# When splits, rests of weights and norms are issued between the score phases of a fused attention and MLP kernel

## The chip, the cores and the metric

The kernel runs on one core of one Trainium2 chip. The metric is the device time of one execution in microseconds (us); lower is better. The runs of the kernel before the change took 1242.66 us in the median of three (1241.65 to 1244.49).

## The reference

`x` is [2048, 512]. An attention branch with 32 query heads of 16 that share one key and one value head, and an MLP with a squared ReLU, are mixed by a gate:

```python
q = (x @ wq).reshape(B, S, H, Dh).transpose(0, 2, 1, 3)   # S = 2048, H = 32, Dh = 16
k = x @ wk; v = x @ wv
scores = einsum("bhqd,bkd->bhqk", q, k) * Dh ** -0.5
a = (softmax(scores) @ v, heads side by side) @ wo
h = relu(x @ w1 + b1) ** 2                                # F = 1792
b = h @ w2 + b2
g = sigmoid((x * gate_w).sum(-1, keepdims=True))
out = g * a + (1 - g) * b
```

## The kernel before

**The products.** Every float32 factor of a large product is split in two, a rounded part (`r`) and the rest (`l = f - r`), and a product of 512 columns is summed from the three partial products r·r, l·r and r·l. A *unit* of work is one such product into one bank of PSUM, 12 matmul slots long (9 or 3 for some). `work()` lists the units: the queries (`q_unit`), the MLP's first layer (`hidden`), its second (`summed`), the output projection, and the last chunk's rows (`onto`). Two units run side by side in the two halves of TensorE's rows: the first half of one unit beside the second half of the unit before. Such a pair is a `Span`.

**The attention** is cut into four chunks of 512 queries and eight groups of four heads, which gives 32 iterations `it` of 32 *score units* (128 keys by 256 queries by four heads), 1024 in all. For a score unit TensorE makes the scores (L761). Most go into a tile `s` that ScalarE reads at once (exp, L798). About every fifth goes into the tile `x`, of which there is a single buffer: VectorE copies it out (L782, `e<-x`), and ScalarE takes the exp later. Until the second of a unit's two copies out of `x` is done, no other use of `x` can start, so TensorE stops at its next matmul into `x`.

**The loop** goes `block(u)`, `phase()`, `context()`. `block` chooses how many score units come next: six, or four where a span of 12 slots is cut into two halves. `phase` emits score matmuls and product matmuls (L1102) on TensorE in an order that a table, `PLANS`, gives for the number of units, the slots, and WHOLE, FIRST or SECOND: `M` is a product slot, `S3` the scores of the phase's unit 3 into `s`, `02` one half (0) of unit 2 into `x`, followed by its copy, and `12` the other. `context` then multiplies exponents by values (L812) for units whose scores were made four units before: 24 matmuls for six units, 16 for four. The instructions of each engine run in the order in which this Python code emits them.

**VectorE's order** is set by a planner. `at_pe`, `at_act` and `at_dve` are clocks that it keeps for the three engines with costs written in the code. Ahead of each copy out of `x`, `spend()` puts on VectorE whatever these clocks say has time: the rest of a weight tile that ScalarE has rounded (`w_rest`, L490; ScalarE's rounding is L495, due at `since`), evictions, items of `divisions`, and `chores`. There are 24 divisions for a pair of iterations (bound L826, compare L829, reciprocal L832, product L833, for six parts of the columns), with `at_act + 10` as the time from which they are ready. Chores are the splits of attention rows (load of `stage` from `oTs` on SyncE, L961; cast and rest, L191 and L192) and of other operands. After a chore that issues a load, `held` keeps the next chore back by 6 us of the planner's time.

A weight tile is loaded by `w_load` (L473, SyncE) into one of two places for each layer: `w2f` and a slice of `stage` alternate for the second layer. A tile is rounded by ScalarE (L495) or VectorE (L481). If a unit begins whose tiles aren't there, `have` makes them at once, burst-wise, and loads them first if it must. A hidden unit is evicted in four operations (L660, L661, L191, L192), a summed one in one (L684).

At the end of an iteration `finish` copies the accumulator (L845, ScalarE) and unpacks it by two DMAs on SyncE (L203, L204); when `it` is even, all divisions that are left are put on VectorE at once. At an iteration's start `q_load` issues eight DMAs on SyncE (L433).

**The norms of q.** For each of the chunk's query groups `qnorm` (L412) sums squares by four small matmuls into the bank of `x`; a root (L347, L348) reads them out. It stands at the start of the phase that follows. That happens four times within the loop.

**The tail.** The last pair of iterations is finished by transposes (`turn`, L876 to L885). Where the sequence of units has nothing ready, a span is empty; the start of a span after it makes TensorE wait for a copy of one column (`peek`, L1125).

Of the kernel before, what the change touches and what calls it, by code (L numbers as in the profile page):

```python
# [22 lines left out]
NC, CH = 4, 512  # L23
NG = 8
NK = S // 128
NF = F // 128
# [6 lines left out]
ROOT = float(0x1fbd1df5 + 0x80000)  # L33
WARM = 10
PARTS = [slice(a, min(a + 86, CH)) for a in range(0, CH, 86)]
LANDS, DIVIDES = 6.0, 10.0
PAIR, CONTEXT, TURN, EXP, COPY, LATE = 0.235, 0.429, 0.36, 0.925, 0.66, 0.3
GROUPS = (0, 1, 2, 3), (4, 5, 6, 7), (8, 9, 10), (11, 12, 13)
AHEAD = 4
WHOLE, FIRST, SECOND = range(3)  # L40
PLANS = {
    (6, 12, WHOLE): ("M 02 S0 M S1 M M M M M S3 M M M S4 12 M M S5", (0, 1, 3, 4, 5, 2)),
    (6, 9, WHOLE): ("S0 M 03 M S1 M M M S2 M M M S4 13 M S5", (0, 1, 2, 4, 5, 3)),
    (6, 6, WHOLE): ("S0 M S1 M 03 M S2 M 13 M S4 M S5", (0, 1, 2, 4, 3, 5)),
    (6, 6, SECOND): ("S0 M S1 M 03 M S2 M 13 M S4 M S5", (0, 1, 2, 4, 3, 5)),
# [117 lines left out]
def mix_kernel(ctx: ExitStack, tc: tile.TileContext, xT, wkv, wq, wo, w12, b1, b2, cst, out):  # L163
# [16 lines left out]
    ok = keep.tile([128, NC * KT * len(PARTS)], F32, name="ok")  # L180
# [46 lines left out]
    with fast, tc.tile_pool(name="at", bufs=1) as at, \  # L227
# [249 lines left out]
        def w_round(half, copy):  # L477
            n = len(rounded[half])
            assert n < room[half]
            rounded[half][n] = [at.tile([128, 512], F32R, name=f"w{half + 1}{x}", bufs=3 + half) for x in "rl"]  # L480
            copy(rounded[half][n][0], wf[half][n])  # L481
            if copy == scalar_copy:
                since[half][n] = act(0.64)
            else:
                since[half][n] = dve(0.46)

# [133 lines left out]
        def spend(until=None):  # L620

            nonlocal held

            def fits(d, ready=0.0):
                return until is None or max(at_dve, ready) + d <= until

            while True:
                due = [i for i in halves() if len(rounded[i]) > len(ws[i])]
                if due and fits(0.68, since[due[0]][len(ws[due[0]])]):
                    w_rest(due[0])  # L630
                elif soon and fits(soon[0][1]):
                    dve(soon[0][1])
                    soon.pop(0)[2]()
                elif divisions and fits(*divisions[0][:2]):
                    d, ready, f = divisions.pop(0)
                    dve(d, ready)
                    f()
                elif chores and fits(chores[0][0], held):
                    d, f = chores.pop(0)
                    dve(d, held if d else 0.0)  # L640
                    if f():
                        held = max(at_dve, at_pe) + 6.0
                else:
                    return

# [46 lines left out]
        def x_again(c):  # L692

            r, l = [xp.tile(sh, F32R, name=f"x{n}again{c}", tag=f"x{n}{c - 2}") for n in "rl"]
            def load(a):
                nc.sync.dma_start(stage()[:, :2], xT[c, 2 * a:2 * a + 2].rearrange("k p s -> p k s"))
                return True

            def part(k):
                split(r[:, k], l[:, k], stage()[:, k % 2])  # L700
                if k == KT - 1:
                    x[c] = r, l

# [97 lines left out]
        def context(acc, us):  # L801

            nonlocal at_pe
            at_pe += 0.12
            while us:
                u, (it, kt, q) = us[0], place(us[0])
                n = 2 if u % 2 == 0 and len(us) > 1 and it < NC * NG - 1 else 1
                at_pe = max([at_pe] + [made[i] + 0.06 for i in us[:n]]) + CONTEXT * n
                us = us[n:]
                cols, mine = slice(q * HC, (q + n) * HC), slice(u % 2 * HC, (u % 2 + n) * HC)  # L810
                for h in range(4):
                    nc.tensor.matmul(acc[h * 32:(h + 1) * 32, cols], v_ext[:, kt],  # L812
                                     es[u // 2][:, h % 2 * 2 + h // 2, mine], start=(kt == 0), stop=(kt == NK - 1),
                                     skip_group_check=True, tile_position=(0, h * 32))
            at_pe += 0.24

        ol = {}
# [17 lines left out]
        def finish(it, acc):  # L835

            c, gr = divmod(it, NG)
            t, u = divmod(gr, 2)
            if it == NC * NG - 2:
                a = at.tile([128, CH], F32, name="al", tag="accs")  # L840
                nc.vector.tensor_copy(a, acc)
                side.append(turn(a, 0, range(4), LAST_OK))
                return
            a = at.tile([128, CH], F32, name="accs")
            nc.scalar.activation(a, acc, AF.Copy)  # L845
            act(0.62, at_pe)
            if u == 0:
                while divisions:
                    divisions.pop(0)[2]()
                ol[c, t] = [at.tile([128, CH], F32, name=n) for n in ("oc", "lc")]  # L850
            o, l = ol[c, t]
            unpack(nc.sync, o[u * 64:u * 64 + 64], l[u * 64:u * 64 + 64], a)
            if u == 1:
                for q, cols in enumerate(PARTS):
                    i = len(PARTS) * (4 * c + t) + q
                    divisions.extend((d, at_act + DIVIDES, f) for d, f in divide(o, l, cols, ok[:, i:i + 1]))

                def done():
# [73 lines left out]
        def o_ready(c):  # L932

            if c == 0 and not wos:
                wos.extend(xp.tile(sh, F32R, name=n, tag=t) for n, t in (("wor", "xr2"), ("wol", "xl2")))

                def load(a):
                    nc.sync.dma_start(stage()[:, :2], wo[a * 256:a * 256 + 256].rearrange("(t p) n -> p t n", p=128))
                    return True

                for t in range(KT):
                    if t % 2 == 0:
                        chores.append((0.0, lambda t=t: load(t // 2)))
                    later(split, wos[0][:, t], wos[1][:, t], stage()[:, t % 2])
            if c > 0:
                ask(c - 1)

        def ask(c, n=KT):
            if c in asked or any((c, t) not in complete for t in range(n)) or c > len(asked):
                return  # L950
            if c and not used[c - 1]:
                return
            asked.add(c)
            tiles = []

            def load(a):
                if a == 0:
                    tiles.extend((keep.tile(sh, F32R, name="orr", tag="r3"), xp.tile(sh, F32R, name="orl", tag="xl3")))
                m = min(2, n - 2 * a)
                i = c * NG + 4 * a  # L960
                nc.sync.dma_start(stage()[:, :m], oTs[i:i + 2 * m].rearrange("(t u) d n -> (u d) t n", u=2))  # L961
                return True
# [12 lines left out]
        def ask_one(c, t):  # L975
# [5 lines left out]
            def load():  # L981
                i = c * NG + 2 * t
                nc.sync.dma_start(stage()[:, :1], oTs[i:i + 2].rearrange("(t u) d n -> (u d) t n", u=2))
                return True

            def part():
                split(osp[c][0][:, t], osp[c][1][:, t], stage()[:, 0])
# [141 lines left out]
        def phase(slots, n, m):  # L1129

            nonlocal scored, evicted, at_pe
            step_aside()
            if narrow:
                used_x[0] = dve(1.3) + 0.06
                qnorm(narrow.pop(0))
            if span.done[0] == 0:
                begin()
            kind = SECOND if span.done[0] else WHOLE if slots == span.slots else FIRST
            text, order = PLANS.get((n, slots, kind)) or plain(n, slots)
            rows = [], []  # L1140
            for item in text.split():
# [40 lines left out]
        def block(u):  # L1182
# [15 lines left out]
        halved, units_left = [0.5], [NC * (NF + 16) + 15 + 12]  # L1198

        acc, us = None, ()  # L1200
        fetch()
# [79 lines left out]
```

## Time and profile before

| | |
|---|---|
| Median of three runs | 1242.66 us (1241.65 to 1244.49) |
| The profiled execution's own time | 1243.74 us |
| Span of the profiled execution | 1242.0 us |
| Mean granted clock of TensorE | 0.992 |
| TensorE matmuls (PE) | 1219.7 us busy, 98% of the span |
| ScalarE (ACT) | 1038.9 us busy, 84% |
| VectorE (DVE) | 767.0 us busy, 62% |
| GpSimd (POOL) | 67.3 us busy, 5% |

Since TensorE is nearly always busy, a shared average says little. The places to look at are the few where the start of one context (L812) stands further from the next than the same pair of steps needs elsewhere, and the rows around them: what TensorE waited for (the bracket at a row's end), and what VectorE was doing ahead of the copy that released it.

### The profile page before, as it was taken

Reading aid. Unit: us, or ns where it says so; the run is one execution under the profiler, and the core shown is the slowest. Engines: PE = TensorE matmul, PEld = TensorE weight load, DVE = VectorE, ACT = ScalarE, POOL = GpSimd, SP = SyncE. Lnnn points to the kernel's source line nnn. Section 1 sums busy time; section 2 is a strip of 40 time slices with the busy share of each in tenths; the row PEclk is TensorE's granted clock in tenths of the full one; section 3 lists DMA queues with packets and bytes.
Section 4 is the critical chain, followed back from the end, with each engine's and each line's share of the span. In section 5 each row is a group of like instructions: output and inputs, shape, how many; then the busy total and the mean of one; then the engine's idle time right before and its main releaser. Section 6 shows DMA issues by size and latency. Waiting matters only on the chain.

```text
span 1242.0 us, 24097 instructions
## 1 busy us (share of the span) xinstructions
PE 1219.7 (98%) x9838; PEld 674.0 (54%) x9839; DVE 767.0 (62%) x1507; ACT 1038.9 (84%) x1151; POOL 67.3 (5%) x87
## 2 busy tenths in 40 slices
PE   9999999999999999999999999999999999999997
PEld 4554555555555545555555556555555555554553
DVE  6765667567485854738477674755838577465543
ACT  6788788888898878888798888888888888887864
POOL 1000120000000110000002001000000000000000
PEclk9999999999999999999999999999999999999989
DMA  6334331211213122102124212112112222300011
GB/s 225 85 106 112 91 94 42 65 57 56 64 61 116 56 82 94 58 21 65 56 82 132 77 41 92 46 48 65 62 67 61 73 65 82 90 31 27 23 51 37
DMA packets 45349, 88.72 MB, mean 71 GB/s; under 512 B 10643, under 2 KB 10899, under 8 KB 44721
## 3 DMA queue, kind: packets, MB, share of 16 engines
q1 hardware_dynamic: 37024, 68.27, 18.2%
q0 software_dynamic: 8064, 18.59, 4.7%
q8 instruction: 79, 1.29, 0.5%
q14 instruction: 38, 0.30, 0.1%
q10 hardware_dynamic: 144, 0.26, 0.1%
HBM read 57.83 MB, written 20.97 MB: 63 GB/s over the span
## 4 chain that ended last, share of the span: by engine, by line
PE 90%; ACT 5%; DVE 2%; DMA 1%; issue 1%; SPq 0%; ACTq 0%; DVEq 0%
PE acc L812 35%; PE mm L1102 31%; PE s L761 16%; PE x L761 5%; ACT e L798 4%; DMA stage<-oTs 1%; PE mm L295 0%; DMA qa<-qs 0%; DVE e L782 0%; PE acc L524 0%; PE mm L199 0%; DVE n L832 0%; ACT w1r L495 0%; DVE tmp L347 0%; SPq L433 0%
## 5 line engine op out<-in xcount | busy, mean ns | idle before, releaser
L798 ACT ACTIVATE e<-s 128x1024 f32<-128x1024 f32 x825 | 786.1, 1025 | 176.8 <-PE s L761 158.7
L812 PE MATMUL acc<-e,v_ext 128*32 128x512 f32 (+1 forms) x4224 | 487.4, 590 | 0.0
L782 DVE COPY e<-x 128x512 f32<-128x512 f32 x398 | 274.6, 690 | 329.2 <-PE x L761 284.5
L761 PE MATMUL s<-qa,k_aug 49*128 49x512 f32 x1650 | 466.4, 414 | 1.8 <-ACT e L798 1.2
L761 PEld LDWEIGHTS s<-qa,k_aug 49*128 49x128 f32 x1650 | 235.8, 185 | 79.5 <-ACT e L798 54.5
L812 PEld LDWEIGHTS acc<-e,v_ext 128*32 128x32 f32 x4224 | 117.2, 110 | 244.6 <-issue 241.3
L1102 PE MATMUL mm<-w2r,hr 64*128 64x512 f32 x896 | 228.5, 402 | 0.0
L798 ACT ACTIVATE e<-e 128x1024 f32<-128x1024 f32 x199 | 211.1, 1061 | 0.4 <-DVE e L782 0.4
L761 PE MATMUL x<-qa,k_aug 49*128 49x512 f32 x398 | 162.9, 409 | 7.8 <-DVE e L782 6.1
L1102 PEld LDWEIGHTS mm<-w2r,hr 64*128 64x128 f32 x896 | 136.0, 186 | 46.3 <-DVE hr L192 15.9
L1102 PE MATMUL mm<-w2l,hr 64*128 64x512 f32 x448 | 144.9, 393 | 0.0
L761 PEld LDWEIGHTS x<-qa,k_aug 49*128 49x128 f32 x398 | 74.3, 187 | 52.2 <-issue 10.9
L1102 PEld LDWEIGHTS mm<-w2l,hr 64*128 64x128 f32 x448 | 80.8, 186 | 6.8
L1102 PE MATMUL mm<-xragain,w1r 64*128 64x512 f32 x224 | 76.8, 418 | 0.2
L1102 PE MATMUL mm<-xr,w1r 64*128 64x512 f32 x224 | 74.1, 417 | 0.3
L1102 PE MATMUL mm<-xlagain,w1r 64*128 64x512 f32 x224 | 74.3, 391 | 0.0
L1102 PE MATMUL mm<-xragain,w1l 64*128 64x512 f32 x224 | 73.3, 392 | 0.0
L1102 PE MATMUL mm<-xl,w1r 64*128 64x512 f32 x224 | 72.4, 392 | 0.0
L1102 PE MATMUL mm<-xr,w1l 64*128 64x512 f32 x224 | 71.4, 393 | 0.0
L832 DVE RECIPROCAL n<-n 128x86 f32<-128x86 f32 x90 | 61.5, 684 | 2.0
L1102 PEld LDWEIGHTS mm<-xragain,w1r 64*128 64x128 f32 x224 | 38.4, 185 | 28.5 <-issue 11.7
L1102 PEld LDWEIGHTS mm<-xr,w1r 64*128 64x128 f32 x224 | 37.5, 185 | 27.5 <-issue 10.4
(162 smaller groups left out, 1178.2 us busy)
## 6 DMA issues: line engine op xcount, KB each, us to landing
stage<-in_w SPq DMA_DIRECT2D x56, 256.0 KB
qa<-qs SPq DMA_DIRECT2D x186, 64.0 KB
w1f<-in_w SPq DMA_DIRECT2D x28, 256.0 KB
w2f<-in_w SPq DMA_DIRECT2D x28, 256.0 KB
qs<-qr SPq DMA_DIRECT2D x16, 256.0 KB
ress<-res POOLq DMA_DIRECT2D x4, 1024.0 KB, 4.9
qs<-ql POOLq DMA_DIRECT2D x15, 256.0 KB, 8.7
oc<-accs SPq DMA_DIRECT2D x30, 128.0 KB
```

The lines of the kernel that those rows point to most:

```text
L761: nc.tensor.matmul(dst.rearrange("p (a n) -> p a n", a=2), k_aug[rows, kt * 128:(kt + 1) * 128], qa[it][rows, :, q * HC:q * HC + HC], star ...
L782: nc.vector.tensor_copy(e_half(u)[:, 2 * r:2 * r + 2], x.rearrange("p (a n) -> p a n", a=2))
L798: nc.scalar.activation(e_half(u), src, AF.Exp, scale=SCALE)
L812: nc.tensor.matmul(acc[h * 32:(h + 1) * 32, cols], v_ext[:, kt], es[u // 2][:, h % 2 * 2 + h // 2, mine], start=(kt == 0), stop=(kt == NK ...
L832: return ((0.23, bound), (0.35, compare), (0.72, lambda: nc.vector.reciprocal(n[0], n[0])), (0.28, lambda: nc.vector.tensor_tensor(o[:, co ...
L1102: nc.tensor.matmul((self.before if r else self).bank, a[p], b[p], start=not r and i == 0, stop=r == 1 and i == len(self.terms[1]) - 1, ski ...
```

## The change

Four edits, all in the order of the work:

1. A constant `SURE` = 0.7 is added to the time at which a weight tile rounded by ScalarE is due. Its rest on VectorE is therefore planned later, often behind a copy where it stood ahead of one, and a tile that would have waited for ScalarE may be rounded on VectorE instead.
2. A chore's function returns how long the next chore is held back: 6 us as before for most loads, 10 us for the loads of attention rows in `ask`. The divisions of the pair (chunk 3, pair 2) are ready after 6 us, the others after 10 as before.
3. `qnorm` is emitted at the end of `context()` rather than at the start of the next phase, and that phase, if whole, uses a new plan `LATER`, in which the first matmul into `x` stands seven items later.
4. A span is not cut into halves where ten score units of the iteration pair are left, nor behind a `qnorm`.

```diff
-LANDS, DIVIDES = 6.0, 10.0
+LANDS, DIVIDES, SURE = 6.0, 10.0, 0.7
...
-WHOLE, FIRST, SECOND = range(3)
+WHOLE, FIRST, SECOND, LATER = range(4)
 PLANS = {
     (6, 12, WHOLE): ("M 02 S0 M S1 M M M M M S3 M M M S4 12 M M S5", (0, 1, 3, 4, 5, 2)),
+    (6, 12, LATER): ("S0 M M S1 M M M 02 M S3 M M M S4 M 12 M M S5", (0, 1, 3, 4, 5, 2)),
...
             if copy == scalar_copy:
-                since[half][n] = act(0.64)
+                since[half][n] = act(0.64) + SURE
...
-                    if f():
-                        held = max(at_dve, at_pe) + 6.0
+                    wait = f()
+                    if wait:
+                        held = max(at_dve, at_pe) + wait
...
+            if narrow:
+                at_pe = max(at_pe + 0.2, used_x[0] + 0.05)
+                qnorm(narrow.pop(0))
+                late.append(True)
+                used_x[0] = dve(1.3, at_pe + 0.2) + 0.06
             at_pe += 0.24
...
-                    divisions.extend((d, at_act + DIVIDES, f) for d, f in divide(o, l, cols, ok[:, i:i + 1]))
+                    divisions.extend((d, at_act + (LANDS if (c, t) == (NC - 1, 2) else DIVIDES), f) for d, f in divide(o, l, cols, ok[:, i:i + 1]))
...
                 nc.sync.dma_start(stage()[:, :m], oTs[i:i + 2 * m].rearrange("(t u) d n -> (u d) t n", u=2))
-                return True
+                return DIVIDES
...
-            if narrow:
-                used_x[0] = dve(1.3) + 0.06
-                qnorm(narrow.pop(0))
             if span.done[0] == 0:
                 begin()
             kind = SECOND if span.done[0] else WHOLE if slots == span.slots else FIRST
+            if late and (n, slots, kind) == (6, 12, WHOLE):
+                kind = LATER
+            late.clear()
...
-            if rest == 8 or rest == 4 or left > 9 and halved[0] >= 1.0 and rest != 6:
+            if rest == 8 or rest == 4 or left > 9 and halved[0] >= 1.0 and rest not in (6, 10) and not late:
```

Because these edits feed the planner's clocks, the order changes far from where they stand. Three places follow, each as the list of an engine's instructions in program order. Lines of the changed kernel lie one to seven above those of the kernel before.

**VectorE, the second load of attention rows of chunk 0** (`stage<-oTs`, some 450 us into the run). The names: `orr` and `orl` are the split parts of attention rows, `res` a summed unit's sum, `w1l` a weight's rest. Before:

```order
L833 TENSOR_TENSOR oc<-oc,n 128x82
L490 TENSOR_TENSOR w1l<-stage,w1r 128x512
L782 COPY e_4948<-x 128x2x256
L191 CAST orr<-stage 128x512
L192 TENSOR_TENSOR orl<-stage,orr 128x512
L782 COPY e_4948<-x 128x2x256
L782 COPY e<-x 128x2x256 x2
L684 SCALAR_TENSOR_TENSOR res_4654<-mm,omg,res_4654 128x512
L191 CAST orr<-stage 128x512
L192 TENSOR_TENSOR orl<-stage,orr 128x512
L782 COPY e<-x 128x2x256
```

After, the same two splits:

```order
L836 SCALAR_TENSOR_TENSOR lc,ok<-n,lc 128x82
L839 RECIPROCAL n<-n 128x82
L840 TENSOR_TENSOR oc<-oc,n 128x82
L192 CAST orr<-stage 128x512
L193 TENSOR_TENSOR orl<-stage,orr 128x512
L784 COPY e<-x 128x2x256
L192 CAST orr<-stage 128x512
L193 TENSOR_TENSOR orl<-stage,orr 128x512
L784 COPY e<-x 128x2x256 x3
```

Before, the second load was issued behind the split in the fourth row, and the split that needs it is the one in the ninth, three copies and one eviction behind. After, the second load is issued in an earlier iteration pair, some 45 rows up, and an iteration's divisions lie between it and the splits.

**TensorE, the second norm of the loop** (some 88 us into the run). `blk` and `sq` belong to the norm; `xr`, `xl`, `wqr`, `wql` are the split factors of a q unit. Ahead of the first row stand the context and three more pairs of the norm, in both kernels. Before:

```order
L412 LDWEIGHTS blk
L412 MATMUL x<-sq_142,blk 32x512
L1102 MATMUL mm<-xr_82,wqr 128x512 x2
L761 MATMUL x<-qa,k_aug 128x512
L761 MATMUL s<-qa,k_aug 128x512 x2
L1102 MATMUL mm<-xl_86,wqr 128x512 x2
```

After:

```order
L413 LDWEIGHTS blk
L413 MATMUL x<-sq_142,blk 32x512
L763 MATMUL s<-qa,k_aug 128x512 x2
L1109 MATMUL mm<-xr_82,wqr 128x512 x2
L1109 MATMUL mm<-xl_86,wqr 128x512 x2
L763 MATMUL s<-qa,k_aug 128x512 x2
L1109 MATMUL mm<-xr_82,wql 128x512 x2
L1109 MATMUL mm<-xr_82,wqr 128x512 x2
L1109 MATMUL mm<-xl_86,wqr 128x512 x2
L763 MATMUL x<-qa,k_aug 128x512
```

The next score into `x` stood one product slot behind the norm, and now stands seven items behind it.

**VectorE, a burst of second-layer weights** (score units 188 to 194, some 255 us into the run; `big` and `hr` are the eviction of a hidden unit, `w2r` and `w2l` the two parts of a weight tile). Before:

```order
L660 TENSOR_SCALAR big<-mm,b1t 128x512
L661 TENSOR_TENSOR big<-big 128x512
L191 CAST hr<-big 128x512
L192 TENSOR_TENSOR hr<-big,hr 128x512
L481 CAST w2r<-w2f 128x512
L490 TENSOR_TENSOR w2l<-w2f,w2r 128x512
L481 CAST w2r<-stage 128x512
L490 TENSOR_TENSOR w2l<-stage,w2r 128x512
L782 COPY e<-x 128x2x256
```

After:

```order
L662 TENSOR_SCALAR big<-mm,b1t 128x512
L663 TENSOR_TENSOR big<-big 128x512
L192 CAST hr<-big 128x512
L193 TENSOR_TENSOR hr<-big,hr 128x512
L482 CAST w2r<-stage 128x512
L491 TENSOR_TENSOR w2l<-stage,w2r 128x512
L482 CAST w2r<-w2f 128x512
L491 TENSOR_TENSOR w2l<-w2f,w2r 128x512
L482 CAST w2r<-stage 128x512
L491 TENSOR_TENSOR w2l<-stage,w2r 128x512
L784 COPY e<-x 128x2x256
```

Two tiles were made between the eviction and the copy, each from its own place; now three are, and the third comes from the same place as the first. Bursts of this kind also stand ahead of score unit 688 (three tiles, `w2f`, `stage`, `w2f`) and of 840 (two, the second of which is loaded by SyncE behind two unpacking and eight query DMAs).

More of the change, by code (lines that the diff above doesn't have):

```diff
@@ L696, in load @@
                 nc.sync.dma_start(stage()[:, :2], xT[c, 2 * a:2 * a + 2].rearrange("k p s -> p k s"))
-                return True
+                return LANDS
             def part(k):
@@ L938, in load @@
                     nc.sync.dma_start(stage()[:, :2], wo[a * 256:a * 256 + 256].rearrange("(t p) n -> p t n", p=128))
-                    return True
+                    return LANDS
                 for t in range(KT):
@@ L961, in load @@
                 nc.sync.dma_start(stage()[:, :m], oTs[i:i + 2 * m].rearrange("(t u) d n -> (u d) t n", u=2))
-                return True
+                return DIVIDES
             def part(t):
@@ L983, in load @@
                 nc.sync.dma_start(stage()[:, :1], oTs[i:i + 2].rearrange("(t u) d n -> (u d) t n", u=2))
-                return True
+                return LANDS
             def part():
@@ L1196, in block @@
             return min(rest, 6), left
-        halved, units_left = [0.5], [NC * (NF + 16) + 15 + 12]
+        late, halved, units_left = [], [0.5], [NC * (NF + 16) + 15 + 12]
         acc, us = None, ()
```

## The prediction

> **What bounds the kernel now.** I read first the page's busy times and the chain that ended last, then the starts of the contexts in TensorE's timeline, then the rows around the late ones.
>
> ```profile
> PE 1219.7 (98%) x9838; PEld 674.0 (54%) x9839; DVE 767.0 (62%) x1507; ACT 1038.9 (84%) x1151; POOL 67.3 (5%) x87
> PE 90%; ACT 5%; DVE 2%; DMA 1%; issue 1%; SPq 0%; ACTq 0%; DVEq 0%
> ```
>
> TensorE sets the end. VectorE matters only in the places where a copy out of `x` comes late. Undisturbed prices come from neighbouring contexts (start, duration, operation; x24 is six units, x16 four):
>
> ```profile
> 236.30 2.78 PE L812 MATMUL acc<-e,v_ext 128*32 128x512 f32 x24
> 241.58 1.93 PE L812 MATMUL acc<-e,v_ext 128*32 128x512 f32 x16
> 245.97 1.92 PE L812 MATMUL acc<-e,v_ext 128*32 128x512 f32 x16
> 252.25 2.78 PE L812 MATMUL acc<-e,v_ext 128*32 128x512 f32 x24
> 259.39 2.78 PE L812 MATMUL acc<-e,v_ext 128*32 128x512 f32 x24
> ...
> 93.81 2.78 PE L812 MATMUL acc<-e,v_ext 128*32 128x512 f32 x24
> 100.45 1.92 PE L812 MATMUL acc<-e,v_ext 128*32 128x512 f32 x16
> 106.24 2.78 PE L812 MATMUL acc<-e,v_ext 128*32 128x512 f32 x24
> ```
>
> From one start to the next: a first half behind six units 5.28, a second half behind four 4.39, a whole span behind four 6.28, a whole behind six 7.14, a six-unit second half behind four 5.79 (100.45 to 106.24). Whatever is over these is a stall. I hold each place that the change touches against them.
>
> **The change, part by part.** *Early weight rests (edit 1).*
>
> ```profile
> DVE w2l L490 <- ACT w2r L495: 49.0, 25, 3.1
> ...
> 98.44 0.69 DVE L490 TENSOR_TENSOR w2l<-w2f,w2r 128x512 fp32r<-128x512 f32 x1 [2.59 <-ACT w2r L495]
> 99.79 0.49 PE L761 MATMUL x<-qa,k_aug 49*128 49x512 f32 x1 [0.89 <-DVE e L782]
> ...
> 146.85 2.78 PE L812 MATMUL acc<-e,v_ext 128*32 128x512 f32 x24
> 152.80 1.92 PE L812 MATMUL acc<-e,v_ext 128*32 128x512 f32 x16
> ```
>
> VectorE waits at 98 us for ScalarE's rounding, the copy behind it is late, and TensorE idles 0.89. The 49.0 us of such waits are mostly idle time that costs nothing; by the contexts only four cost anything: 93.81 to 100.45 is 6.64, 1.36 over 5.28; the last, 146.85 to 152.80, is 5.95, 0.67 over; the four together 3.9.
>
> *Norms (edits 3 and 4).* The first and the last of four:
>
> ```profile
> 52.06 2.78 PE L812 MATMUL acc<-e,v_ext 128*32 128x512 f32 x24
> 58.20 1.92 PE L812 MATMUL acc<-e,v_ext 128*32 128x512 f32 x16
> 157.20 1.92 PE L812 MATMUL acc<-e,v_ext 128*32 128x512 f32 x16
> 163.00 1.92 PE L812 MATMUL acc<-e,v_ext 128*32 128x512 f32 x16
> ...
> 88.42 0.40 PE L412 MATMUL x<-sq,blk 128*32 128x512 bf16 x4
> 89.63 0.50 PE L761 MATMUL x<-qa,k_aug 49*128 49x512 f32 x1 [0.39 <-DVE tmp L347]
> ```
>
> These are 6.14 and 5.80, so 0.86 and 1.41 over; four come to 4.6. The score into `x` waits for the root's reading (0.39 in the last row). Behind `LATER`'s seven items this wait is covered; the small matmuls themselves stay, at most 0.40 each (first row of the last two). Of 3.9 + 4.6 = 8.5 I leave 2.1 (four norms, 1.6, and 0.5 for a wait whose rest may still stand ahead): **−6.4**. If a rest's cover is gone again, one such place costs the 0.7 to 1.4 above.
>
> *Attention rows of chunk 0 (edit 2).*
>
> ```profile
> 452.04 1.92 PE L812 MATMUL acc<-e,v_ext 128*32 128x512 f32 x16
> 461.64 3.66 PE L812 MATMUL acc<-e,v_ext 128*32 128x512 f32 x24
> 469.66 2.78 PE L812 MATMUL acc<-e,v_ext 128*32 128x512 f32 x24
> ...
> 459.82 0.61 PE L761 MATMUL x<-qa,k_aug 49*128 49x512 f32 x1 [2.19 <-DVE e L782]
> ...
> 460.00:465.00 5.00, 5.00 (x31) 1.61 (x30) 2.81 (x5) 2.49 (x3) 0.00 (x0) 0.66 0.01 2
> ```
>
> 9.60 against 6.28 and 8.02 against 7.14: 4.2 over. Only 2.19 is the gap; the other 2.0 is lost behind it, where the granted clock is 0.66 and the context takes 3.66 in place of 2.78. The order puts the second load an iteration pair's work earlier: **−4.2**.
>
> [...]
>
> *Attention rows of chunk 3.*
>
> ```profile
> 1117.88 2.78 PE L812 MATMUL acc<-e,v_ext 128*32 128x512 f32 x24
> 1125.30 3.35 PE L812 MATMUL acc<-e,v_ext 128*32 128x512 f32 x16
> 1131.33 1.92 PE L812 MATMUL acc<-e,v_ext 128*32 128x512 f32 x16
> ...
> 1124.63 0.50 PE L761 MATMUL x<-qa,k_aug 49*128 49x512 f32 x1 [1.67 <-DVE e L782]
> ```
>
> 7.42 against 5.28, and 6.03 against 4.39: 3.8 over, of it a gap of 1.67. With 10 in place of 6 the split stands one half-phase (4.4) later, and the gap was shorter than that: **−3.8**. Late next are two splits behind one eviction, which just fit.
>
> *The flush of divisions* at an even iteration.
>
> ```profile
> 593.83 1.92 PE L812 MATMUL acc<-e,v_ext 128*32 128x512 f32 x16
> 599.63 3.34 PE L812 MATMUL acc<-e,v_ext 128*32 128x512 f32 x16
> ```
>
> 5.80 against 4.39, and a context 1.42 longer: 2.8. At this iteration (14) the order now has six items ahead of a phase of nine slots, whose first copy isn't urgent: **−2.8**.
>
> *The tail.*
>
> ```profile
> 1192.13 1.93 PE L812 MATMUL acc<-e,v_ext 128*32 128x256 f32 x32
> 1199.36 3.64 PE L812 MATMUL acc<-e,v_ext 128*32 128x256 f32 x32
> 1206.05 1.93 PE L812 MATMUL acc<-e,v_ext 128*32 128x256 f32 x32
> ```
>
> 7.23 and 6.69, where a second half behind four needs about 4.4: 5.1 over. An empty span brings a `peek` here, together with `turn`. With the pair's divisions ready at 6, the rows come a phase earlier, and the order has no empty span at this place; the transposes stay (1.5 of the 5.1), and a later `peek` is dropped (0.4): **−4.0**.
>
> *Halving (edit 4).* Counting spans in the two orders: three spans cut into four and six (5.28 + 5.79 = 11.07) and three whole ones (7.14) become six cut into four and four (8.80, a tenth over 2 × 4.39 by the first half). 54.6 to 52.8: **−1.8**.
>
> *What it adds: bursts of weights.* In the kernel before, the burst that the order shows costs nothing:
>
> ```profile
> 252.27 0.74 DVE L660 TENSOR_SCALAR big<-mm,b1t 128x512 f32<-128x512 f32 x1
> 254.84 0.42 DVE L481 CAST w2r<-w2f 128x512 fp32r<-128x512 f32 x1
> 255.29 0.69 DVE L490 TENSOR_TENSOR w2l<-w2f,w2r 128x512 fp32r<-128x512 f32 x1
> ...
> oTs<-oc POOLq DMA_DIRECT2D x15, 256.0 KB, 2.3
> ```
>
> The eviction takes 2.57 (252.27 to 254.84), a cast with its rest 1.07 (254.84 to 255.91, both rows overlapping their neighbours). After, the third tile of the burst at unit 188 goes into the place of the first. Its load can't start before the first rest is done, 0.02 + 2.57 + 1.07 = 3.7 behind the context's start. The trace doesn't show such a load by itself; the nearest row is a DMA of the same 256 KB, 2.3. So it lands at about 6.1, its cast and rest end at 7.2, the copy at 7.9. TensorE wants `x` at 2.78 + 2.30 = 5.1: the stalled first half above starts its wait at 1124.63 − 1.67 = 1122.96, which is 2.30 behind the end of the context before it. Gap 2.9, and 2.0 of clock: **+4.9**. At unit 688 it is the same burst ahead of a whole phase, which starts its wait at 459.82 − 2.19 = 457.63, so 3.7 behind its start: 6.5 against 7.9, gap 1.5, with clock **+3.5**. At unit 840 the load stands on SyncE's queue behind ten others:
>
> ```profile
> 971.46 4.43 SPq L433 DMA_DIRECT2D qa<-qs  x8
> ```
>
> Those eight take 4.43 to issue. I put its landing 3.7 behind the phase's start, the copy's end at 5.5, against 3.7: gap 1.8, **+3.8**. Below, all three are bounded by zero (the tile is there in time, as in the burst of before); above, by a landing of 5.85, as long as the query loads ahead of chunk 0's rows took by the chain: 3.5 more each, +10.5 together.
>
> *The flush again.* At iteration 8 the order now has a cast, seven division operations and a rest between two copies, ahead of a second half of four units, the situation that cost 2.8 at 593.83 with about the same work: **+2.8**. Small shifts that I can't follow: +1.0. The ten more VectorE operations and six fewer on ScalarE lie beside TensorE's 98%.
>
> **Sum.** −6.4 − 4.2 − 3.8 − 2.8 − 4.0 − 1.8 = −23.0; +4.9 + 3.5 + 3.8 + 2.8 + 1.0 = +16.0; net −7.0. From the profiled execution's own 1243.74 that gives 1236.7; it stands 1.1 above the median of its kernel's runs (1242.66), so a median of some 1236.
>
> **The rivals.** *The loads are hidden.* If the third tiles are loaded in time, the three bursts cost what the one of 254.84 did, nothing: 12.2 less, about 1224; with one of them left, about 1228. For it: that burst; against it: a place that holds the first tile can't take the third.
>
> *The gaps cost no clock.* If the clock stays up behind gaps of 1.5 to 2.9, the three bursts cost 6.0 less (3 × 2.0) and the flush 1.4, and some 1229 results. Against it stand the clock of 0.66 behind 2.19 above and the contexts of 3.35 and 3.34 behind the other two. [...]
>
> *Slower: late loads.* One mechanism at the three places of 188, 688 and 840: weight loads on demand land late, since they share queue and engines with query loads. Each us of landing beyond 2.3 is a us of TensorE's gap at each place. Three us each make +9 and 1245, so from a landing of about 5.4 the change is slower. For it: the query loads' 5.85; against it: 2.3 for the same size, and at 188 and 688 no other load is known to stand ahead.
>
> *Little change.* The waits are only moved: a burst a us longer each and half of the tail's gain missing (2.0) give some +5, so 1241.
>
> **How the numbers follow.** Forecast (1231 to 1240): 0.46. Hidden loads (below 1231): 0.15. No loss of clock (1229): 0.05. Little change (1240.2 to 1245.1): 0.20. Late loads (above 1245): 0.14. A measurement of this kernel can tell about 0.2%, 2.5 us, from no change. Faster is the first three, 0.66; same 0.20; slower 0.14. The range leaves some 0.1 below and 0.1 above: 1228 to 1246.
>
> **What would show it.** Right: contexts near 88 and 160 us at their regular distances but for about 0.3; no row of `x` that waits near 460, 596 and 1124; three new gaps of 1.5 to 2.9 ahead of scores into `x` behind `w2r`, `w2l`, near 255, 830 and 1010, with a granted clock below 0.9 behind them. Wrong: a gap of 2 us with the clock at 1.00, a `w2r` cast in a burst that waits for no DMA, a new `peek` in the tail, or a stall in a place that I haven't named.

## The result: slower, not faster

The changed kernel took 1248.49 us in the median of eight runs (1244.89 to 1252.67), the kernel before 1243.0 (1241.65 to 1247.31, eight runs). The ratio is 1.0044, with a 95% interval of 1.0024 to 1.0065: slower by some 5.5 us, or 0.4%, where 7 less was forecast. The profiled execution of the changed kernel took 1246.41 with a span of 1244.6, so it lies 2.1 under its own median, and the one of before 0.7 over its own.

The page of the changed kernel, with the busy times and the chain that ended last:

```profile
PE 1216.1 (98%) x9839; PEld 669.9 (54%) x9839; DVE 772.1 (62%) x1517; ACT 1036.8 (83%) x1145; POOL 65.1 (5%) x87
...
PE 89%; DVE 4%; DMA 3%; ACT 3%; issue 1%; SPq 0%; ACTq 0%; DVEq 0%
```

TensorE is as busy as before and still sets the end. The chain now has 3% of DMA in place of 1%, and 4% of VectorE in place of 2%.

To find where the time went I took, for each phase and each context, its duration less the median of its kind in the kernel before, and added these excesses up by score units (a calculation over all rows, in us):

| | before | changed | difference | forecast |
|---|---|---|---|---|
| start of the first context of the loop | 36.1 | 38.4 | +2.3 | 0 |
| regular prices of all phases and contexts | 1165.9 | 1163.8 | −2.1 | −1.8 |
| excess, units 0 to 110 | 9.3 | 12.3 | +3.0 | −6.4 |
| 110 to 280 | 0.5 | 7.1 | +6.6 | +4.9 |
| 280 to 480 | 4.3 | 1.5 | −2.8 | −1.4 |
| 480 to 680 | 3.4 | 0.7 | −2.7 | −2.8 |
| 680 to 860 | 0.3 | 5.0 | +4.7 | +7.3 |
| 860 to 980 | 3.7 | 0.0 | −3.7 | −3.8 |
| 980 to the end | 7.7 | 5.0 | −2.7 | −4.0 |

The differences come to +2.6, as the spans do (what the rows leave out of the spans, 10.8 at the very end, is the same in both). The forecast's +1.0 for small shifts has no row. The other rows came within 2.6 of the forecast. The first 110 units did not: two large stalls stand there that I had not named.

**The first, near 70 us.** The changed kernel's timeline, ScalarE, VectorE and TensorE together (start, duration, operation; in brackets the idle time ahead and what ended it):

```profile
65.46 0.69 DVE L784 COPY e<-x 128x512 f32<-128x512 f32 x1 [1.52 <-PE x L763]
68.51 0.39 PE L763 MATMUL x<-qa,k_aug 49*128 49x512 f32 x1
70.72 1.02 ACT L800 ACTIVATE e<-s 128x1024 f32<-128x1024 f32 x1 [1.69 <-PE acc L814]
71.64 0.21 ACT L519 ACTIVATE g<-z 128x16 f32<-128x16 f32 x1
71.88 0.18 DVE L520 TENSOR_SCALAR g<-g 128x16 f32<-128x16 f32 x1 [5.73 <-ACT g L519]
72.58 0.63 DVE L784 COPY e<-x 128x512 f32<-128x512 f32 x1
74.58 0.50 PE L1109 MATMUL mm<-xr,wqr 64*128 64x512 f32 x2 [2.27 <-DVE ql L393]
```

VectorE's next instruction is the first operation of the mixing gate, which reads an exp that ScalarE makes. On ScalarE that exp stands behind an exp of scores that itself waits for a context (1.69). So VectorE stands still from 66.15 to 71.88. The scores in `x` were there by 68.9; their copy begins at 72.58, the eviction of a q unit comes behind it, and TensorE idles 2.27. In the kernel before, the same operations fell at 60 us, where VectorE idled only 1.85 for them, and the next context stood at most 0.3 late:

```profile
60.62 0.18 DVE L519 TENSOR_SCALAR g<-g 128x16 f32<-128x16 f32 x1 [1.85 <-ACT g L518]
```

**The second, near 90 us**, in the rows of SyncE, VectorE and TensorE:

```profile
77.32 8.33 SPq L434 DMA_DIRECT2D qa<-qs  x8
85.94 0.36 SPq L474 DMA_DIRECT2D w1f<-in_w  x1
...
91.79 0.43 DVE L482 CAST w1r<-w1f 128x512 fp32r<-128x512 f32 x1 [4.97 <-DMA w1f<-in_w]
93.48 0.50 PE L763 MATMUL x<-qa,k_aug 49*128 49x512 f32 x1 [3.56 <-DVE e L784]
94.38 3.35 PE L814 MATMUL acc<-e,v_ext 128*32 128x512 f32 x16
```

Eight query loads take 8.33 us to issue. At the same place in the kernel before it was 6.20:

```profile
71.68 6.20 SPq L433 DMA_DIRECT2D qa<-qs  x8
```

A weight load waits behind them on SyncE and lands 5.85 after its issue. VectorE was to cast that tile ahead of a copy, waits 4.97, and TensorE idles 3.56; the context behind takes 3.35 in place of 1.92.

**The bursts that I had named** are there. The one at unit 188:

```profile
260.24 0.33 SPq L474 DMA_DIRECT2D stage<-in_w  x1
262.83 0.43 DVE L482 CAST w2r<-stage 128x512 fp32r<-128x512 f32 x1 [1.56 <-DMA stage<-in_w]
264.64 0.49 PE L763 MATMUL x<-qa,k_aug 49*128 49x512 f32 x1 [3.11 <-DVE e L784]
265.30 3.60 PE L814 MATMUL acc<-e,v_ext 128*32 128x512 f32 x16
271.38 1.92 PE L814 MATMUL acc<-e,v_ext 128*32 128x512 f32 x16
```

The load on demand takes 2.6, the gap is 3.11 (2.9 forecast), and the place costs 5.2 (4.9 forecast). At the bursts ahead of units 688 and 840 the excess is 2.3 and 2.4 (3.5 and 3.8 forecast), since the granted clock was 1.00 there in this execution (830 to 850 and 1008 to 1030 us).

**The stalls that were to go** have gone. Contexts at the rows of chunk 0 and of chunk 3 in the changed kernel:

```profile
460.69 1.92 PE L814 MATMUL acc<-e,v_ext 128*32 128x512 f32 x16
465.10 1.92 PE L814 MATMUL acc<-e,v_ext 128*32 128x512 f32 x16
469.48 1.93 PE L814 MATMUL acc<-e,v_ext 128*32 128x512 f32 x16
475.75 2.78 PE L814 MATMUL acc<-e,v_ext 128*32 128x512 f32 x24
...
1127.27 2.78 PE L814 MATMUL acc<-e,v_ext 128*32 128x512 f32 x24
1132.54 1.93 PE L814 MATMUL acc<-e,v_ext 128*32 128x512 f32 x16
1136.93 1.92 PE L814 MATMUL acc<-e,v_ext 128*32 128x512 f32 x16
```

They lie 4.41, 4.38, 6.27, then 5.27 and 4.39 apart, which are the regular distances. And edit 1 does what it says; the list of waits has this row, in place of 49.0 us in 25 waits:

```profile
DVE w2l L491 <- ACT w2r L496: 0.8, 2, 0.5
```

### The profile page after: what moved, and what is told of

Its sections match the earlier page's. It is cut to its first block, busy times and chain, and to the rows that moved or that the text cites. A ratio compares the mean times of both kernels' runs of the same rounds, so it can differ in the third digit from the quotient of the medians.

```text
span 1244.6 us, 24154 instructions
## 1 busy us (share of the span) xinstructions
PE 1216.1 (98%) x9839; PEld 669.9 (54%) x9839; DVE 772.1 (62%) x1517; ACT 1036.8 (83%) x1145; POOL 65.1 (5%) x87
## 3 DMA queue, kind: packets, MB, share of 16 engines
q8 instruction: 79, 1.29, 0.4%
## 4 chain that ended last, share of the span: by engine, by line
PE 89%; DVE 4%; DMA 3%; ACT 3%; issue 1%; SPq 0%; ACTq 0%; DVEq 0%
PE acc L814 35%; PE mm L1109 31%; PE s L763 16%; PE x L763 5%; ACT e L800 2%; DVE e L784 1%; DMA qa<-qs 1%; DMA stage<-in_wo 0%; DMA xf<-in_xT 0%; DMA w1f<-in_w 0%; DMA stage<-in_w 0%; PE mm L296 0%; PE mm L200 0%; DVE big L662 0%; DVE big L663 0%
## 5 line engine op out<-in xcount | busy, mean ns | idle before, releaser
L784 DVE COPY e<-x 128x512 f32<-128x512 f32 x404 | 279.0, 691 | 391.7 <-PE x L763 349.6
L800 ACT ACTIVATE e<-e 128x1024 f32<-128x1024 f32 x202 | 214.4, 1061 | 0.8 <-DVE e L784 0.8
L763 PE MATMUL x<-qa,k_aug 49*128 49x512 f32 x404 | 164.4, 407 | 10.8 <-DVE e L784 9.8
L1109 PEld LDWEIGHTS mm<-xragain,w1r 64*128 64x128 f32 x224 | 38.4, 185 | 28.6 <-issue 9.2
```

Source lines behind the costliest of these rows:

```text
L763: nc.tensor.matmul(dst.rearrange("p (a n) -> p a n", a=2), k_aug[rows, kt * 128:(kt + 1) * 128], qa[it][rows, :, q * HC:q * HC + HC], star ...
L784: nc.vector.tensor_copy(e_half(u)[:, 2 * r:2 * r + 2], x.rearrange("p (a n) -> p a n", a=2))
L800: nc.scalar.activation(e_half(u), src, AF.Exp, scale=SCALE)
L1109: nc.tensor.matmul((self.before if r else self).bank, a[p], b[p], start=not r and i == 0, stop=r == 1 and i == len(self.terms[1]) - 1, ski ...
```

## The experiments

All ratios compare with runs of the kernel before on the same chip, whose medians lay between 1242.19 and 1242.7. "Less than the changed kernel" compares with the 1248.49 above, which comes from eight runs that spread over 7.8 us. Theory: the change wins and loses in separate places; edits 1 and 2 win, edit 3 brings the two stalls near 70 and 90 us, edit 4 the three bursts. The first rival: the lost time is spread, or moves on to the next place when one is mended.

### Mending one place of the changed kernel at a time

**The gate behind the next copy** (a_gate).

```diff
-        ... + [(14, 2.0, gate)]
+        ... + [(14, 2.0, lambda: gates.append(gate))]
...
+        gates = []
...
             copied[u] = copied.get(u, 0) + 1
+            while gates:
+                gates.pop()()
```

> The changed kernel, with the gate (two exps on ScalarE, four small operations on VectorE) emitted behind the next copy out of x instead of ahead of it; the planner's clocks are untouched, so all else keeps its order. Theory (the gate is a stall of its own): in the changed kernel's trace VectorE idles 5.73 us for ScalarE's exp of the gate near 72 us, the copy behind it is late, and the contexts there lie 2.8 us further apart than elsewhere; without it about 1248.5 - 2.8 = 1245.7. Rival (ScalarE is late there anyway, because the context before holds its exps back): under 0.5 us is gained, 1248.

Measured: 1246.09, ratio 1.0021 (1.0004 to 1.0037). The median is near the theory's, but the trace doesn't bear it out: VectorE still waits, and so does the eviction behind.

```profile
70.97 0.17 DVE L520 TENSOR_SCALAR g<-g 128x16 f32<-128x16 f32 x1 [2.26 <-ACT g L519]
73.07 0.50 PE L1112 MATMUL mm<-xr,wqr 64*128 64x512 f32 x2 [1.67 <-DVE ql L393]
```

The excess there fell from 2.8 to 2.25 only, so most of the 2.4 between the medians is not this place's. What this run settles is that the copy wasn't the whole of it.

**The weight load from another queue** (a_w1load).

```diff
-                nc.sync.dma_start(wf[half][n], ...)
+                eng = nc.gpsimd if (half, n) == (0, 2) else nc.sync
+                eng.dma_start(wf[half][n], ...)
```

> The changed kernel, with one load of a first-layer weight tile (the third) issued from GpSimd's queue instead of SyncE's, where it stands behind eight query loads that took 8.33 us to issue. Theory (the late load is the stall near 91 us, a gap of 3.56 us and a slower clock behind it, 5.3 us in all): about 1248.5 - 5.3 = 1243. Rival (the load is late because the DMA engines are busy, whatever queue issues it): the cast still waits, and the time stays within 1 us of 1248.5.

Measured: 1242.33, ratio 0.9982 (0.9965 to 1.0000), 6.2 less than the changed kernel. The cast's wait, 4.97, is now this:

```profile
86.61 0.43 DVE L483 CAST w1r<-w1f 128x512 fp32r<-128x512 f32 x1 [0.39 <-DMA w1f<-in_w]
```

The query loads still take 8.25 us to issue. The weight load now leaves at 76.61, some 9 us earlier, and is in time although it takes 10.0 to land (5.85 from SyncE). So standing behind the query loads is what had made it late; that its transfer was quick is not shown, rather the reverse.

**A third place for a tile at unit 188** (a_third).

```diff
+                elif half == 1 and n in (7, 9):
+                    place = stage()[:, 0 if n == 7 else 3]
```

> The changed kernel, with the third second-layer tile of the burst near score unit 188 loaded into a free part of the stage tile, so that its load need not wait for the first tile's rest. Theory (load on demand 1.6 us of the 3.11 us gap, the rest of the gap is the burst's own length): the gap near 262 us shrinks to about 1.45 us. If such a gap still loses clock (2 us), 1.7 us less, 1246.8; if a gap of 1.45 keeps the clock, 3.7 less, 1244.8. Rival (the split work of three tiles alone sets the copy): no change, 1248.5.

Tile 7 takes the free part of `stage`, tile 9 goes back to the old place. Measured: 1243.87, ratio 0.9999 (0.9981 to 1.0017), 4.6 less, where 1.7 to 3.7 was expected. In its profile the gap is 1.46, as expected, and the context behind it still took 3.08:

```profile
262.25 0.49 PE L765 MATMUL x<-qa,k_aug 49*128 49x512 f32 x1 [1.46 <-DVE e L786]
262.90 3.08 PE L816 MATMUL acc<-e,v_ext 128*32 128x512 f32 x16
```

So the load on demand made up 1.65 of the gap, and the length of the burst the rest. The excess between 110 and 280 units fell by 1.6, the lower of the two values expected; the other 3 us between the medians aren't explained by this place and lie within the spread of the runs.

**All three** (a_all3).

> The three edits together. Theory (three independent stalls): 2.8 + 5.3 + 1.7 to 3.7 = 9.8 to 11.8 less than 1248.5, about 1237 to 1239, so faster than the kernel before the change at 1243. Rival (what is gained in one place is lost in the next, since the loads behind come as much earlier): half of it or less, 1243 to 1246.

Measured: 1238.26, ratio 0.9954 (0.9939 to 0.9969), 10.2 less than the changed kernel, within the theory's 9.8 to 11.8 and out of the rival's range. That the three are independent doesn't follow: the gate's wait is still 2.26 here, as in a_gate, and the next run shows that two of the stalls were one chain. Nor is the rival quite gone: in this profile the excess between 680 and 860 units is 9.7 (5.0 in the changed kernel), in part because the clock didn't hold at the burst ahead of unit 688 (granted 0.5 from 833.9; the context at 836.99 took 4.59 in place of 2.78).

**The gate's exps a span earlier** (a_gate2). The operations on VectorE stay.

```diff
-        ... + [(14, 2.0, gate)]
+        ... + [(13, 0.0, gate_exps), (14, 2.0, gate)]
```

> The changed kernel, with the two exps of the gate on ScalarE emitted one span earlier than their four VectorE operations, which stay where they are. Moving the VectorE part behind the copy had taken only 0.5 us off that place, since the eviction behind still waited for ScalarE. Theory (VectorE stands still there because ScalarE reaches the gate's exps late): the wait for them and the 2.8 us near 70 us go, about 1245.7. Rival (the eviction is late there for another reason): contexts keep their distance, under 0.7 us gained, 1248.

Measured: 1240.42, ratio 0.9979 (0.9970 to 0.9988): 8 less, where 2.8 was expected. The reason is in SyncE's rows:

```profile
74.92 4.96 SPq L434 DMA_DIRECT2D qa<-qs  x8
79.99 0.36 SPq L474 DMA_DIRECT2D w1f<-in_w  x1
```

The eight query loads take 4.96 now, not 8.33, and the weight load is in time: there is no wait for it any more. The two stalls were one chain. How the late gate slowed the query loads can in part be read from what SyncE waited for in the changed kernel (us in total, times, longest):

```profile
SPq L434 <- DMA oc<-accs: 1.9, 1, 1.9
SPq L434 <- DMA lc<-accs: 0.8, 1, 0.8
```

The seventh and the eighth query load stood until the two unpacking DMAs, issued just ahead of the eight, had landed. These 2.7 are most of the difference of 3.4. All seven profiled kernels that have the gate's stall show both waits (1.8 to 2.3, and 0.8), and their eight loads took 7.73 to 8.37 to issue; the two with edit 3 but without the stall show neither, and took 4.91 and 4.96. Why the unpacking landed so late was not tried by itself. GpSimd's write of a query tile may be the reason; it is issued behind the eviction, 2.5 ahead of the query loads in the changed kernel (first row) and 5 ahead in a_gate2, with the gate in time (second row):

```profile
74.82 0.69 POOL L355 DMA_DIRECT2D qs<-ql  x1 [10.50 <-DVE ql L393]
...
69.96 0.69 POOL L355 DMA_DIRECT2D qs<-ql  x1 [6.65 <-DVE ql L393]
```

Such writes take 8.2 us to land in the median. That one in flight slows the other transfers isn't shown; it is an estimate from these times.

### Each edit alone, on the kernel before

Edit 1 alone (s_sure) adds `SURE` and nothing else:

> The kernel before the change with edit 1 alone (0.7 added to the due time of weight tiles that ScalarE rounds). Its order keeps the bursts, the norms and the rows as before; early rests move behind their copies, and the flush at iteration 14 falls from eleven items to six. Theory (each edit's effect is that of its own places): the four early waits of 3.9 us and the flush of 2.8 go, so 1243 - 6.7 = 1236. Rival (rests held back are late for the products instead): within 1.5 us of 1243.

Measured: 1236.59, ratio 0.9947 (0.9928 to 0.9966). The number is near the theory's, but in part by luck. VectorE's waits are gone (those for `w2l` are 1.3 us in all, 49.0 before), and so is the stall of the flush; but the excess in the first 110 units fell by 0.7 only, where the four early waits were to give 3.9. The rest came from the rows of chunk 0 and from the tail, which the new order happened to clear. Only one of the four, near 99 us, was a late copy (1.36 before, 0.72 now). At the others no copy is late, and TensorE's only idle time is for ScalarE's exps (0.25, 0.49 and 0.46, of excesses of 0.7, 1.2 and 0.7), which edit 1 doesn't touch. The first row shows this for the last of them, in the kernel before; the second is what is left near 99 us with edit 1:

```profile
152.38 0.50 PE L761 MATMUL s<-qa,k_aug 49*128 49x512 f32 x2 [0.46 <-ACT e L798]
...
100.58 0.50 PE L761 MATMUL s<-qa,k_aug 49*128 49x512 f32 x2 [0.48 <-ACT e L798]
```

Edit 2 alone (s_wait) has the returned waits and the 6 for the pair of chunk 3:

> The kernel before the change with edit 2 alone (chores behind loads of attention rows held back 10 instead of 6, the divisions of chunk 3, pair 2 ready at 6). Theory: the stalls at the rows of chunk 0 (4.2) and chunk 3 (3.8) go, and the tail loses two waits for a peek (2.2 to 4.0), so 10 to 12 less, 1231 to 1233. Rival (the splits only fall into another copy's way): 4 less or under, 1239 and above.

Measured: 1232.92, ratio 0.9925 (0.9896 to 0.9954), as the theory says; no stall is left at the rows of chunk 0 and of chunk 3.

Edit 3 alone (s_norm) has `qnorm` behind the context, the plan `LATER`, and no halving behind it:

> The kernel before the change with edit 3 alone (norms behind the contexts, the plan for the phase after, no halving there). Theory (the gate's wait and the late weight load near 72 and 91 us belong to this edit, since it alone moves them): 2.1 gained at the norms, 2.8 and 5.3 lost, 1243 + 6 = 1249. Rival (both come from edit 1 or 4): 2 less, 1241.

Measured: 1247.32, ratio 1.0037 (1.0018 to 1.0056). Both stalls are there:

```profile
70.56 0.17 DVE L520 TENSOR_SCALAR g<-g 128x16 f32<-128x16 f32 x1 [5.73 <-ACT g L519]
90.89 0.43 DVE L482 CAST w1r<-w1f 128x512 fp32r<-128x512 f32 x1 [5.36 <-DMA w1f<-in_w]
```

Edit 4 without its part behind a norm (s_ten):

```diff
-... halved[0] >= 1.0 and rest != 6:
+... halved[0] >= 1.0 and rest not in (6, 10):
```

> The kernel before the change with edit 4 in part (no halving where ten score units are left). In its order stand the same three bursts with loads on demand as in the changed kernel, ahead of units 188, 688 and 840. Theory (the bursts belong to this edit): 1.8 gained by the spans, 5.2 + 2.3 + 2.4 lost, 1243 + 8 = 1251. Rival (the bursts need edit 1's later rests as well): 1.8 less, 1241.

Measured: 1247.18, ratio 1.0023 (1.0004 to 1.0041). It lost less than expected because it also happened to shift the rows of chunk 0 and the tail: its excess is 1.9 between 280 and 480 units and 4.6 in the tail (4.3 and 7.7 before). The burst at 188 is as in the changed kernel:

```profile
262.04 0.79 PE L761 MATMUL x<-qa,k_aug 49*128 49x512 f32 x1 [3.08 <-DVE e L782]
263.19 3.64 PE L812 MATMUL acc<-e,v_ext 128*32 128x512 f32 x16
```

Alone the four make −5.7, −9.4, +5.0 and +4.9, together −5.2, but the whole change is +5.5. The gains don't add, since edits 1, 2 and 4 each clear the same places: the excess between 280 and 480 units is 0.7, 0.2 and 1.9 in place of 4.3, and in the tail 4.6, 5.1 and 4.6 in place of 7.7. The losses stand at places of their own, edit 3's in the first 110 units and edit 4's behind them, so they do add.

### Undoing and combining

**The changed kernel without the exception at ten units** (u_ten).

```diff
-... rest not in (6, 10) and not late:
+... rest != 6 and not late:
```

> The changed kernel with edit 4's new exception undone (spans may be halved where ten score units are left; the one behind a norm stays). In its order the bursts ahead of units 188, 688 and 840 are gone. Theory (those bursts are the price of that exception): 6.6 and 4.7 us of the excess between 110 and 280 and between 680 and 860 score units go, 1.8 of spans come back, about 1248.5 - 9.5 = 1239. Rival (the bursts only mark places where the order would stall anyway): 1246 to 1250.

Measured: 1234.39 (1234.0 to 1235.69), ratio 0.9937 (0.9923 to 0.9950): 14 less than the changed kernel. Its excess is 0.4 between 110 and 280 units and 0.5 between 680 and 860. The profiled spans differ by 10.7 (1244.6 and 1233.9), near the 9.5 expected; the other 3 or so lie in the spread of the changed kernel's runs.

**Edits 1 and 2** (b_12).

> The kernel before the change with edits 1 and 2 together. Alone they gave 1236.6 and 1232.9, but both of them removed the stalls at the rows of chunk 0 and in the tail. Theory (shared places count once): edit 1 adds to edit 2 an early wait of 0.7 and the flush of 1.6 to 2.1, so 1232.9 - 2.7 = 1230. Rival (the gains add up): 1243 - 5.7 - 9.4 = 1228 or less.

Measured: 1230.29, ratio 0.9905 (0.9888 to 0.9921). The theory's value: shared places count once. The rival's 1228 lies just outside the interval (1228.3 to 1232.4).

**Edits 1, 2 and 3 with both places of edit 3 mended** (b_123): `gate_exps` a span earlier, the one weight load from GpSimd, no exception at ten.

> Edits 1, 2 and 3 with both places of edit 3 mended: the gate's exps a span earlier, and the third first-layer weight tile loaded from GpSimd's queue. No exception at ten units. Theory (the norms behind the contexts are a gain once what they moved is mended): in the first 110 score units 12.3 - 5.3 - 2.8 = 4.2 us of excess in place of the 8.6 that edits 1 and 2 leave, about 1230 - 4.4 = 1225.6. Rival (the plan for the phase behind a norm costs what the norm saves): 1229 to 1231.

Measured: 1228.08 (1227.86 to 1228.41), ratio 0.9886 (0.9871 to 0.9901), the fastest of all: 14 us less than the kernel before, 20 less than the changed one. Over b_12 it gains 2.2, half of what the theory said, so between it and its rival. In its profile the phases behind the four norms still cost 0.75 to 0.88 each, and a new wait of 1.2 stands near 70 us.

## Why the prediction was wrong

- **What bounds the kernel** held in the main: TensorE sets the end. That VectorE matters only by late copies out of `x` was too narrow. In the changed kernel TensorE also waits 2.27 for the eviction of a q unit, and 1.27 and 1.07 for the cast of a weight tile at the two later bursts; and it waits for ScalarE's exps, as above.
- **The failed step is that of the early rests and the norms, −6.4, and in it the norms (edit 3).** I asked what the move does at the four norms, and counted shifts elsewhere at +1.0. In fact it moved the gate's operations on VectorE from 60 us, where ScalarE was at hand, to 66, where ScalarE was held up (2.8), and the query write behind it, and with that a weight load (5.3): 8.1 together, shown by s_norm, a_gate2 and a_w1load; only the link from the query write to the slow loads is argued. I had looked at how long VectorE's queue was ahead of each copy. I hadn't asked, for each row in it, when its operand would be ready on another engine.
- **The same step was misread and mis-sized besides.** Of the 3.9 for four early waits edit 1 alone took 0.7 (s_sure): I had put all four down to VectorE's wait for the rounding, but at three of them no copy is late, and TensorE waits for ScalarE's exps instead. The excess of the first 110 units is still 8.6 with edits 1 and 2 (9.3 before). In the changed kernel, with edits 3 and 4 beside them, two of 0.7 remain, near 105 and 113 us, in place of the 0.5 forecast. A phase behind a norm takes 5.06 on average, not 4.43, so four cost 2.5 (1.6 forecast).
- **A wait I hadn't named at all** lies beyond the first 110 units: near 176 us VectorE waits 2.57 for a load of the output weights (row below) ahead of a copy, which with the phase behind it makes 1.7. s_wait, s_sure and s_norm have no such excess there (0.4 to 0.5 in the whole region), nor has u_ten, where the same wait is 0.36. So it too comes with edit 4's exception at ten units.

```profile
175.99 0.43 DVE L192 CAST wor<-stage 128x512 fp32r<-128x512 f32 x1 [2.57 <-DMA stage<-in_wo]
```

- **The rows of chunk 0 and 3, the flush at iteration 14:** right, within 0.2 at each where the table can be read.
- **The tail:** right in kind, −2.7 in place of −4.0; a `peek` near 1219 costs 1.3.
- **The three bursts:** right in place and cause; u_ten shows that edit 4's exception brings them. In this profile 5.2, 2.3 and 2.4; forecast 4.9, 3.5 and 3.8. The difference at the second and third is the clock that I put at 2.0 each: the granted clock was 1.00 there. The flush at iteration 8 cost about 1.3 (2.8 forecast), for the same reason (granted 1.00 from 378 to 394 us). At these three places the rival "the gaps cost no clock" was right.
- **Halving:** −2.1 with all regular prices (−1.8 forecast).
- **The rival that came nearest** was "late loads". Its mechanism (a weight load behind query loads, landing in 5.85) is what happened, but at a tile of the first layer near 90 us, not at the three bursts, where loads landed in about 2.6. I gave it 0.14.
- **What the sum left out:** the start before the loop, 2.3 later in this profile. In the fourteen profiles here the first context began between 36.1 and 41.5 us, though nothing ahead of it was changed. In the kernel before, where the granted clock was 1.00 up to there, it began at 36.1; in the changed kernel, where it was 0.50 from 33.29 to 36.70, at 38.4. How much of the 2.3 is the clock's was not tried. The changed kernel's eight runs, too, differ in their mean granted clock: 0.996 in the one of 1244.89, 0.988 in the one of 1252.67.

## What to carry to other kernels

When a change feeds a planner's clocks, compare the whole order, and ask of every row that moved not only how long it takes but when its operands are ready on the other engines and queues; a row of 0.2 us can hold an engine for 5.7. Gains that several edits make at one place count once, while losses at different places add up, so it pays to run each edit alone. A transfer that is issued late can cost twice: by itself, and by what is queued behind it, as when eight query loads took 8.33 us to issue in place of 4.96 and the weight load behind them kept a cast waiting for 4.97.

## What was not expected of the hardware

Whether a gap of TensorE costs clock isn't decided by its length alone. The burst at unit 188 left gaps of 3.11, 3.05, 1.46 and 1.44 in four profiles; what tells is the context behind each. For 3.11 (the changed kernel) and 1.46 (a_third) the rows stand above, with contexts of 3.60 and 3.08. For 3.05 (a_w1load):

```profile
259.36 0.50 PE L764 MATMUL x<-qa,k_aug 49*128 49x512 f32 x1 [3.05 <-DVE e L785]
260.02 1.92 PE L815 MATMUL acc<-e,v_ext 128*32 128x512 f32 x16
```

And for 1.44 (a_all3):

```profile
256.48 0.49 PE L767 MATMUL x<-qa,k_aug 49*128 49x512 f32 x1 [1.44 <-DVE e L788]
257.13 1.92 PE L820 MATMUL acc<-e,v_ext 128*32 128x512 f32 x16
```

A gap of 3.11 was followed by a context of 3.60 and one of 3.05 by the regular 1.92; 1.46 by 3.08, and 1.44 by 1.92.

Here are 3.41 us of the changed kernel with the gap of 3.11, and those behind them (stretch, its length, busy times of TensorE's matmuls, its weight loads, VectorE, ScalarE and GpSimd, then the granted clock, share and rate of the DMA engines):

```profile
261.98:265.39 3.41, 0.74 (x7) 0.38 (x11) 2.52 (x5) 0.20 (x1) 0.00 (x0) 1.00 0.46 119
265.40:268.80 3.40, 3.40 (x16) 0.50 (x16) 1.49 (x3) 1.97 (x2) 0.00 (x0) 0.50 0.62 195
```

TensorE idles 2.67 in the first, and the second has half the clock. All gaps of TensorE over 1 us behind the first 45 us of both kernels, with the granted clock behind each:

| kernel, row behind the gap | gap | granted clock behind it |
|---|---|---|
| changed, 93.48 | 3.56 | 0.50 from 94.73 to 98.14 |
| changed, 264.64 | 3.11 | 0.50 from 265.40 to 268.81 |
| changed, 74.58 | 2.27 | 1.00 from 74.25 to 81.07 |
| before, 459.82 | 2.19 | 0.50 from 460.05 to 463.46 |
| before, 1124.63 | 1.67 | 0.50 from 1125.65 to 1129.06 |
| before, 598.73 | 1.37 | 0.50 from 600.00 to 603.41 |
| before, 1195.94 (tail) | 1.29 | 0.50 from 1197.33 to 1204.15 |
| changed, 842.92 | 1.27 | 1.00 from 830 to 850 |
| changed, 1019.52 | 1.07 | 1.00 from 1008 to 1030 |
| changed, 385.86 | 1.05 | 1.00 from 378 to 394 |

The clock stayed up behind a gap of 2.27 and fell behind one of 1.29. What decides isn't shown by these runs. The stretches at half clock in the table lasted 3.41 us each, the one in the tail 6.82; 3.41 at half clock loses at most 1.7 of TensorE's work, an estimate from these figures. So the 2.0 us per gap in the forecast was somewhat high, and it was lost behind some gaps only. Fewer stalls also gave narrower runs (0.55 us over four runs of b_123, with a mean granted clock of 0.997 or 0.998 in each).
